# Attention scores on two 64-row tiles of the PE array instead of the full array with a block-diagonal K

## The chip, the cores and the metric

One core of one Trainium2 chip runs the whole kernel. The metric is device time in microseconds, the median of several executions. Engine names are those of the profile: PE is the matrix engine, PEld its weight loads, DVE, ACT and POOL the three element-wise engines, SP the engine that issues DMA.

## The reference, cut to what matters

```python
k_p = k.reshape(B, H, Sp, 8, D).mean(axis=3)            # B=8, H=8, Sp=72, D=64
v_p = v.reshape(B, H, Sp, 8, D).mean(axis=3)
scores = (q @ k_p.transpose(0, 1, 3, 2)) / sqrt(D)      # q: (8, 8, 576, 64)
attn = softmax(scores)                                  # over 72 pooled keys
x = (attn @ v_p) as (4608, 512)
out = gelu_tanh(x @ w_in) @ w_out                       # 512 -> 2048 -> 512
```

The head dimension is 64, half of the 128 rows of the PE array. That is what the change is about. The MLP after the attention is by far the larger part of the work.

## The kernel before

The kernel works through nine groups of 512 tokens: 512 tokens of each of the eight batches, and one remainder group made of the last 64 tokens of all eight. While PE runs the MLP of one group, the attention of the next is woven in at fixed steps of the MLP by hooks. One **score group** is the scores of 128 tokens and 8 heads. Two heads share a full-array matmul: the stationary operand is q of a pair of heads (128 rows), and the moving operand is a block-diagonal K, half of it zeros.

```python
kbd = consts.tile([128, B, HP, 2, Sp], BF16, name="kbd")        # zeroed once with a memset

def scores(g, j):
    sc = psum.tile([128, 2, MAIN], F32, name="sc", tag="sc", bufs=2)       # two banks
    for pr in range(HP):                                                   # 4 pairs of heads
        o = sc[:, pr // 2, 2 * Sp * (pr % 2):2 * Sp * (pr % 2) + 2 * Sp]
        if g < B:
            nc.tensor.matmul(out=o, lhsT=qT[:, j, pr, :], rhs=kbd[:, g, pr] ..., start=True, stop=True)
        else:                                          # remainder group: 64 tokens of two batches
            for half in range(2):
                p0 = 64 * half
                nc.tensor.matmul(out=o[p0:p0 + 64], lhsT=qT[:, j, pr, p0:p0 + 64],
                                 rhs=kbd[:, 2 * j + half, pr] ..., start=True, stop=True)

def exps(g, j):      # ACT: e = exp(sc / 64), 128 x 576
def norm(g, j, eng): # DVE: den = sum, r = 1/den; eb = e * r in bf16
...
# steady state: step 0 to 63 are the matmuls with w_in, 64 to 127 those with w_out
at(hooks, [67, 69, 78, 82][j], scores, n, j)
at(hooks, [67, 69, 78, 82][j], exps, n, j)
# first MLP
at(hooks, 16, first_t, 2)      # PE transposes of e, then a DVE copy
at(hooks, 32, first_t, 3)
at(hooks, 42, first_v)         # fourth cast of w_in on DVE, then the values
```

The softmax here doesn't subtract the row's maximum and nothing guards it: scores larger than these inputs give would overflow.

## Time and profile before

| what | before |
|---|---|
| median time | 301.14 us (301.05 to 301.31, 3 runs) |
| span of the profile | 299.3 us |
| PE busy, share of the span | 97% |
| one steady period (one group of 512 tokens) | 30.36 us, PE busy throughout |
| score group on PE, ordinary / remainder | 0.25 us / 0.47 us |

The lines are in the prediction below. How to read them: in the steady state PE has no gap at all, so the period is a sum of PE's slots, and anything that PE need not do is time gained. A slot is the distance between the starts of two neighbouring matmuls. Durations of single matmuls in the profile are modelled and longer than a slot, because matmuls are pipelined. At the start of the program PE waits for loads and casts, and there the sum of PE's work is not the measure.

### The profile page before, as it was taken

What the parts mean: (1) busy time and instruction counts of PE and PEld (TensorE: products, weight loads), DVE (VectorE), ACT (ScalarE), POOL (GpSimd) and SP (SyncE); (2) the same over time, 40 slices, a digit from 0 to 9 for tenths busy, and PEclk for the clock granted to TensorE, in tenths of its full rate; (3) what the DMA queues carried; (4) which work ended last, traced back from release to release, by engine and by line L of the source; (5) the groups of instructions that cost most, each with busy time, mean ns of one, the idle gap of its engine ahead of it and who ended that gap; (6) DMA issues with size and microseconds to landing.
All of it is one profiled execution on the core that took longest, in us unless ns stands there. A gap on an engine that the chain in (4) does not pass through costs nothing.

```text
span 299.3 us, 4581 instructions
## 1 busy us (share of the span) xinstructions
PE 290.7 (97%) x1734; PEld 151.6 (51%) x1734; DVE 146.7 (49%) x241; ACT 158.2 (53%) x242; POOL 55.5 (19%) x71
## 2 busy tenths in 40 slices
PE   7869999999999999999999999999999999999996
PEld 7748844445444544454445444544444544444444
DVE  6895769164706570648073807381639100920012
ACT  1477783667157715672477246724773267426500
POOL 3252033230400240024012400240024000100000
PEclk9999999999999999999999999999999999999999
DMA  7999997995699459947993599049944800351012
GB/s 235 357 387 338 384 350 132 343 279 158 135 279 250 145 127 271 269 146 126 261 297 134 119 249 301 4 107 249 276 147 101 164 36 2 79 114 37 0 70 70
DMA packets 73221, 56.32 MB, mean 188 GB/s; under 512 B 45808, under 2 KB 55408, under 8 KB 73200
## 3 DMA queue, kind: packets, MB, share of 16 engines
q1 hardware_dynamic: 73056, 55.98, 68.2%
q8 instruction: 13, 0.21, 0.3%
q10 hardware_dynamic: 144, 0.07, 0.1%
q14 instruction: 8, 0.07, 0.1%
HBM read 36.70 MB, written 9.44 MB: 154 GB/s over the span
## 4 chain that ended last, share of the span: by engine, by line
PE 91%; DMA 3%; DVE 2%; SPq 1%; POOL 1%; issue 0%; POOLq 0%
PE mm L296 41%; PE mm L301 41%; PE xo L266 4%; DMA q_sb<-in_q_dram 3%; PE sc L208 2%; PE mm L329 1%; POOL eb L231 1%; SPq L98 1%; PE xo L272 1%; PE tp L193 1%; PE sc L213 0%; DVE w_in_b L80 0%; PE tp L240 0%; DVE w_out_b L80 0%; POOL q_b L80 0%; PE xo L255 0%
## 5 line engine op out<-in xcount | busy, mean ns | idle before, releaser
L301 PE MATMUL mm<-w_out_b,gT 128*128 128x512 bf16 x560 | 128.6, 379 | 0.5 <-DVE w_out_b L80 0.5
L296 PE MATMUL mm<-xT,w_in_b 128*128 128x512 bf16 (+1 forms) x640 | 127.6, 358 | 0.5 <-DVE xT L80 0.5
L298 ACT ACTIVATE gT<-mm 128x512 bf16<-128x512 f32 (+1 forms) x160 | 88.4, 555 | 47.0 <-PE mm L296 45.9
L296 PEld LDWEIGHTS <-w_in_b 128*128 128x128 bf16 x640 | 62.2, 98 | 62.6 <-issue 0.5
L301 PEld LDWEIGHTS <-gT 128*128 128x128 bf16 x560 | 53.4, 98 | 59.7 <-DVE w_out_b L80 0.7
L80 DVE COPY osb<-mm 128x512 f32<-128x512 f32 (+2 forms) x37 | 24.3, 658 | 62.9 <-PE mm L301 60.8
L78 ACT CAST xT<-xo 128x1024 bf16<-128x1024 f32 (+1 forms) x18 | 16.6, 966 | 56.8 <-PE xo L266 49.1
L228 DVE TENSOR_REDUCE den<-e 128x8 f32<-128x576 f32 x36 | 26.5, 736 | 38.0 <-ACT e L221 37.9
L148 POOL TENSOR_TENSOR vbd<-kvb,vmask 128x256 bf16<-128x256 bf16 (+2 forms) x40 | 21.2, 553 | 113.5 <-DVE kvb L130 113.4
L128 DVE TENSOR_TENSOR kv<-kv 128x1024 f32<-128x1024 f32 (+3 forms) x20 | 22.4, 1118 | 29.7 <-DMA kv<-in_v_dram 27.7
L231 DVE TENSOR_TENSOR eb<-e,r 128x576 bf16<-128x576 f32 x28 | 27.2, 970 | 1.0
L221 ACT ACTIVATE e<-sc 128x576 f32<-128x576 f32 x36 | 22.5, 650 | 9.6 <-ACT e L221 4.0
L231 POOL TENSOR_TENSOR eb<-e,r 128x576 bf16<-128x576 f32 x8 | 10.1, 1266 | 71.5 <-ACT e L221 41.1
L80 POOL CAST q_b<-q_sb 128x2048 bf16<-128x2048 f32 (+1 forms) x7 | 15.0, 2147 | 4.1 <-DMA q_sb<-in_q_dram 4.1
L208 PEld LDWEIGHTS <-qT 128*128 128x128 bf16 x128 | 10.1, 98 | 7.0 <-ACT qT L78 0.6
L208 PE MATMUL sc<-kbd,qT 128*128 128x144 bf16 x128 | 13.2, 226 | 0.2 <-ACT qT L78 0.2
L266 PE MATMUL xo<-eT,vbd 128*128 128x512 bf16 x56 | 13.2, 379 | 0.0
L129 DVE TENSOR_TENSOR kv<-kv 128x512 f32<-128x512 f32 (+3 forms) x20 | 12.8, 640 | 0.7
L410 PE MATMUL warm<-identb 128*128 128x128 bf16 x112 | 9.1, 249 | 1.4 <-POOL vmask L398 1.4
L494 ACT ACT_TABLE_LOAD x8 | 10.3, 1283 | 0.1
L80 DVE COPY kbd<-kTd 64x288 bf16<-64x288 bf16 x12 | 5.6, 467 | 8.3 <-DMA kTd<-kvb 8.2
L314 ACT ACT_TABLE_LOAD x7 | 9.0, 1283 | 0.1
(55 smaller groups left out, 99.5 us busy)
## 6 DMA issues: line engine op xcount, KB each, us to landing
out_dram<-osb SPq DMA_DIRECT2D x31, 256.0 KB, 6.7
kv<-in_k_dram SPq DMA_DIRECT2D x7, 1024.0 KB, 6.5
q_sb<-in_q_dram SPq DMA_DIRECT2D x7, 1024.0 KB, 5.9
kv<-in_v_dram SPq DMA_DIRECT2D x7, 1024.0 KB, 9.9
w_in_s<-in_moe_w_in_dram SPq DMA_DIRECT2D x4, 1024.0 KB, 13.0
w_out_s<-in_moe_w_out_dram SPq DMA_DIRECT2D x4, 1024.0 KB, 13.8
out_dram<-osb SPq DMA_DIRECT2D x9, 128.0 KB, 2.3
kv<-in_k_dram SPq DMA_DIRECT2D x2, 512.0 KB, 3.9
```

Of the source, the lines that this page charges most:

```text
L78: eng.copy(out=out, in_=in_)
L80: eng.tensor_copy(out=out, in_=in_)
L128: add(out=t[:, :, 0:4, :], in0=t[:, :, 0:4, :], in1=t[:, :, 4:8, :], op=ALU.add)
L148: eng.tensor_tensor(out=vbd[p0:128, b, n0:n1, :].rearrange("p (c r) (hh d) -> p c (r hh) d", c=max(m, 1), d=D), in0=kvb[p0:128, 4 + c0:4 + ...
L208: nc.tensor.matmul(out=o, lhsT=qT[:, j, pr, :], rhs=kbd[:, g, pr].rearrange("d hh s -> d (hh s)"), start=True, stop=True)
L221: nc.scalar.activation(out=e.rearrange("p (x h) s -> p x (h s)", x=2), in_=sc[:, :, 0:4 * Sp], func=ACT.Exp, scale=1.0 / 64.0)
L228: nc.vector.reduce_sum(out=den, in_=e, axis=AX.X)
L231: eng.tensor_tensor(out=eb[:, j, 128 * 5 - W:].rearrange("p (h s) -> p h s", s=Sp), in0=e, in1=r.unsqueeze(2).to_broadcast([128, H, Sp]), ...
L266: nc.tensor.matmul(out=xo[:, i, :], lhsT=vbd[:, g, n, :], rhs=eT[:, :, c, :], start=(x == 0), stop=(x == 1))
L296: nc.tensor.matmul(out=hp[:, 0:c1 - c0], lhsT=w_in_b[:, ko, fo * 128:(fo + 1) * 128], rhs=st[g]["xT"][:, ko, c0:c1], start=(ko == 0), stop ...
L298: nc.scalar.activation(out=gT[:, fo, c0:c1], in_=hp[:, 0:c1 - c0], func=ACT.Gelu_apprx_tanh)
L301: nc.tensor.matmul(out=o, lhsT=gT[:, fo, r * 128:(r + 1) * 128], rhs=w_out_b[:, fo, :], start=(fo == 0), stop=(fo == FO - 1))
```

## The change

The intent: half of each score matmul multiplies zeros. The PE array can be used as two tiles of 64 rows, with the even head of a pair on one and the odd head on the other at the same time. Then K needs no zeros, and a pair of heads takes 72 columns instead of 144. The two tiles are kept from writing one PSUM bank together (the prediction says on what that rests): even heads go to one bank and odd heads to the other, and the normalisation puts the heads back in order as it writes. Three hooks of the first MLP move as well. The core of the diff:

```diff
-    kbd = consts.tile([128, B, HP, 2, Sp], BF16, name="kbd")
+    kh = consts.tile([128, B, HP, Sp], BF16, name="kh")
...
         for pr in range(HP):
-            o = sc[:, pr // 2, 2 * Sp * (pr % 2):2 * Sp * (pr % 2) + 2 * Sp]
-            if g < B:
-                nc.tensor.matmul(out=o, lhsT=qT[:, j, pr, :], rhs=kbd[:, g, pr] ..., start=True, stop=True)
...
+            for hh in range(2):
+                h0 = 64 * hh
+                o = sc[:, hh, Sp * pr:Sp * pr + Sp]
+                if g < B:
+                    nc.tensor.matmul(out=o, lhsT=qT[h0:h0 + 64, j, pr, :], rhs=kh[h0:h0 + 64, g, pr],
                                      start=True, stop=True)
+                else:
+                    for p0 in (0, 64):
+                        nc.tensor.matmul(out=o[p0:p0 + 64], lhsT=qT[h0:h0 + 64, j, pr, p0:p0 + 64],
+                                         rhs=kh[h0:h0 + 64, 2 * j + p0 // 64, pr], start=True, stop=True)
...
-        eng.tensor_tensor(out=eb[...].rearrange("p (h s) -> p h s", s=Sp), in0=e, ...)
+        eng.tensor_tensor(out=eb[...].rearrange("p (pr hh s) -> p hh pr s", hh=2, s=Sp), in0=e, ...)
...
-    nc.vector.memset(kbd, 0.0)
...
-    at(hooks, 16, first_t, 2)
-    at(hooks, 32, first_t, 3)
-    at(hooks, 42, first_v)
+    at(hooks, 28, first_t, 2)
+    at(hooks, 38, first_t, 3)
+    at(hooks, 48, first_v)
```

More of the change, by code (lines that the diff above doesn't have):

```diff
@@ L184, in k_spread @@
             src = st[b]["kT"][p0:p0 + 64, 0:W].rearrange("d (pr hh s) -> d hh pr s", hh=2, s=Sp)[:, hh]
-            copy(engs[hh], kbd[p0:p0 + 64, b, :, hh, :], src)
+            copy(engs[hh], kh[p0:p0 + 64, b], src)
     def qT_tile(g):
@@ L205, in scores @@
         for pr in range(HP):
-            o = sc[:, pr // 2, 2 * Sp * (pr % 2):2 * Sp * (pr % 2) + 2 * Sp]
-            if g < B:
-                nc.tensor.matmul(out=o, lhsT=qT[:, j, pr, :], rhs=kbd[:, g, pr].rearrange("d hh s -> d (hh s)"),
-                                 start=True, stop=True)
-            else:
-                for half in range(2):
-                    p0 = 64 * half
-                    nc.tensor.matmul(out=o[p0:p0 + 64], lhsT=qT[:, j, pr, p0:p0 + 64],
-                                     rhs=kbd[:, 2 * j + half, pr].rearrange("d hh s -> d (hh s)"),
+            for hh in range(2):
[3 more added lines that the diff above has]
+                    nc.tensor.matmul(out=o, lhsT=qT[h0:h0 + 64, j, pr, :], rhs=kh[h0:h0 + 64, g, pr],
                                      start=True, stop=True)
+                else:
+                    for p0 in (0, 64):
+                        nc.tensor.matmul(out=o[p0:p0 + 64], lhsT=qT[h0:h0 + 64, j, pr, p0:p0 + 64],
+                                         rhs=kh[h0:h0 + 64, 2 * j + p0 // 64, pr], start=True, stop=True)
         st[g][("sc", j)] = sc
@@ L219, in exps @@
         sc = st[g].pop(("sc", j))
-        e = work.tile([128, H, Sp], F32, name="e", bufs=4)
-        nc.scalar.activation(out=e.rearrange("p (x h) s -> p x (h s)", x=2), in_=sc[:, :, 0:4 * Sp],
+        e = work.tile([128, 2, HP, Sp], F32, name="e", bufs=4)
+        nc.scalar.activation(out=e.rearrange("p hh pr s -> p hh (pr s)"), in_=sc[:, :, 0:4 * Sp],
                              func=ACT.Exp, scale=1.0 / 64.0)
@@ L226, in norm @@
         e = st[g][("e", j)]
-        den = work.tile([128, H], F32, name="den")
+        den = work.tile([128, 2, HP], F32, name="den")
         nc.vector.reduce_sum(out=den, in_=e, axis=AX.X)
-        r = work.tile([128, H], F32, name="r")
+        r = work.tile([128, 2, HP], F32, name="r")
         nc.vector.reciprocal(out=r, in_=den)
-        eng.tensor_tensor(out=eb[:, j, 128 * 5 - W:].rearrange("p (h s) -> p h s", s=Sp), in0=e,
-                          in1=r.unsqueeze(2).to_broadcast([128, H, Sp]), op=ALU.mult)
+        eng.tensor_tensor(out=eb[:, j, 128 * 5 - W:].rearrange("p (pr hh s) -> p hh pr s", hh=2, s=Sp),
+                          in0=e, in1=r.unsqueeze(3).to_broadcast([128, 2, HP, Sp]), op=ALU.mult)
     def eT_tile(g):
```

## The prediction

> **What bounds the kernel now.** I read the page top down: engine shares, slices, chain. Then I read one period of the steady state in the windows view, and then the timeline of PE around each kind of score group, because the change acts there.
>
> ```profile
> PE 290.7 (97%) x1734; PEld 151.6 (51%) x1734; DVE 146.7 (49%) x241; ACT 158.2 (53%) x242; POOL 55.5 (19%) x71
> PEclk9999999999999999999999999999999999999999
> PE mm L296 41%; PE mm L301 41%; PE xo L266 4%; DMA q_sb<-in_q_dram 3%; PE sc L208 2%; PE mm L329 1%; POOL eb L231 1%; SPq L98 1%; PE xo L272 1%; PE tp L193 1%; PE sc L213 0%; DVE w_in_b L80 0%; PE tp L240 0%; DVE w_out_b L80 0%; POOL q_b L80 0%; PE xo L255 0%
> ...
> 115.81:146.17 30.36, 30.36 (x154) 14.20 (x152) 15.68 (x24) 16.54 (x24) 6.03 (x7) 1.00 0.78 200
> ```
>
> The reader is to see that PE is the bound, at full clock, and that scores (L208, L213) are under 3% of the chain. In one steady period of 30.36 us PE is busy for all 30.36 while DVE and ACT have half of it free: the period is 64 + 64 matmuls of 512 columns and 8 of the values at 0.216 us (13.81 us for 64 in the chain in order of time), 29.35 us, plus four score groups of 0.25 us, 1.0 us. So whatever the change does to the time PE needs for a score group appears one for one in the total, and whatever it does to DVE, ACT or POOL there is hidden. The start is different: PE waits there, and the change also moves hooks there.
>
> What a score group costs PE is read from starts, since ends of matmuls are modelled:
>
> ```profile
> 100.01 0.59 PE L301 MATMUL mm<-w_out_b,gT 128*128 128x512 bf16 x2
> 100.44 0.41 PE L208 MATMUL sc<-kbd,qT 128*128 128x144 bf16 x4
> 100.69 0.59 PE L301 MATMUL mm<-w_out_b,gT 128*128 128x512 bf16 x2
> ...
> 220.52 0.81 PE L301 MATMUL mm<-w_out_b,gT 128*128 128x512 bf16 x3
> 221.26 0.44 PE L213 MATMUL sc<-kbd,qT 128*64 128x144 bf16 x8
> 221.64 0.60 PE L301 MATMUL mm<-w_out_b,gT 128*128 128x512 bf16 x2
> ```
>
> ```profile
> 32.69 0.52 PE L174 MATMUL kT<-identb,kvb 128*128 128x128 bf16 x5
> 33.00 0.09 PEld L174 LDWEIGHTS <-kvb 64*128 64x128 bf16 x1
> 33.13 0.10 PEld L296 LDWEIGHTS <-w_in_b 128*128 128x128 bf16 x1
> 33.14 0.28 PE L296 MATMUL mm<-xT,w_in_b 128*128 128x256 bf16 x1
> ...
> 34.02 0.39 PE L193 MATMUL tp<-identb,q_b 128*128 128x128 bf16 x4
> 34.24 0.27 PE L296 MATMUL mm<-xT,w_in_b 128*128 128x256 bf16 x1
> ...
> 234.73 2.03 PE L272 MATMUL xo<-eT,vbd 128*128 128x64 bf16 x64
> 236.60 0.60 PE L301 MATMUL mm<-w_out_b,gT 128*128 128x512 bf16 x2
> ```
>
> First fence: an ordinary group (full array, four matmuls of 144 columns) takes 100.69 - 100.44 = 0.25 us, 62.5 ns each. The remainder group (L213) uses 64-column tiles. PE could have begun it at 220.52 + 3 x 0.216 = 221.17; the next full-array matmul starts at 221.64. That is 0.47 us, though two tiles side by side need only four slots of 62.5 ns, 0.25 us: **0.22 us are lost** on the way into the tile shape and out of it. Second fence: the fifth K transpose has 64 rows (64*128), which is the very shape that the change uses. Four full transposes take 0.22 us (34.02 to 34.24), and a 64-column matmul takes 1.87/64 = 0.029 us (234.73 to 236.60), so five should take 0.25. They take 33.14 - 32.69 = 0.45: **0.20 us are lost**. The weight load at 33.00 comes some 0.09 us after the fourth transpose has streamed, and the next full-array load waits again. No semaphore explains it: the operand was ready at 32.66 by the DVE rows.
>
> **What the Trainium skill says.** "TensorEngine Tiling (Array Packing)", Key Properties: "Mode switching requires drain", for a change of mode and not of tile alone. The trace agrees, with 0.20 and 0.22 us for a visit. The same page, Gotcha 1: different row tiles must not write one PSUM bank at once; hence the layout with even heads in one bank and odd heads in the other. No run yet shows it. "TensorE: Matmul & The Clock Gate", Back-to-back issue gap: about N/2.4 + 2.5 ns for each warm matmul. The trace agrees at 144 columns (62.5) and at 64 (29). For 72 columns it gives an estimate of 32.5 ns. The same page, Part 3: matmuls on different row groups start about 4 ns apart. No run here shows this for rows; for columns the remainder group agrees, since its eight matmuls fit only if they run in pairs.
>
> **The change part by part.** (1) Ordinary score groups. Four full matmuls of 144 columns become eight of 64 rows and 72 columns, with eight weight loads. In pairs on the two row tiles they need 4 x 32.5 = 0.13 us, plus the visit, 0.20 to 0.22: about 0.34 us for 0.25, so **+0.09 us a group**. The half that concurrency saves (0.12 us) is less than one visit costs, because each group stands alone between full-array matmuls. Of the 32 ordinary groups four are in the prologue, and two more (at 37.32 and 37.67) stand just ahead of a wait of 0.50 us of PE for the w_out_b cast, which takes in their extra. 26 x 0.09 to 0.10 = **+2.5 us**.
>
> (2) Remainder groups, four. They pay for a visit already. Sixteen matmuls on four 64x64 tiles, four at a time: 4 x 32.5 + 0.22 = 0.35 for 0.47: -0.1 each, **-0.4 us** at best.
>
> (3) The memset of kbd goes (1.98 us of DVE at 1.35). DVE then waits 0.87 us for the first K load anyway: 0.
>
> (4) exp reads the same two times 288 columns. The normalisation writes with a four-dimensional pattern: the same elements on DVE, off the chain in the steady state: 0. The copies of K become contiguous: hidden.
>
> (5) Prologue. Each of the four groups is later by about 0.1; the first feeds a dense DVE chain, the last an ACT copy that PE needs at 19.5: **+0.1 us**.
>
> (6) The hooks. The first e transpose moves from step 16 to 28, the second from 32 to 38.
>
> ```profile
> 22.38 0.45 PE L240 MATMUL tp<-identb,eb 128*128 128x128 bf16 x5 [1.19 <-POOL eb L231]
> 22.67 1.91 PE L296 MATMUL mm<-xT,w_in_b 128*128 128x256 bf16 x16
> 24.42 0.44 PE L240 MATMUL tp<-identb,eb 128*128 128x128 bf16 x5
> 24.82 0.39 PE L296 MATMUL mm<-xT,w_in_b 128*128 128x256 bf16 x2
> ```
>
> This looks like a gain of 1.19 us, PE's wait for the POOL normalisation: 12 matmuls of 0.109 us now fill it. But step 32 needs the third w_in cast, which POOL does right after (22.83 to 24.76, started by a DMA). In the kernel before, PE reaches step 32 at 24.82, just behind that cast. After the change PE gets to step 32 at about 23.1 and waits for the same cast until 24.8. So the wait moves rather than goes, and the second transposition (0.28 us), which used to lie ahead of this join, now lies behind it: **+0.3 us**.
>
> Sum: 2.5 - 0.4 + 0.1 + 0.3 = +2.5 us, 301.1 + 2.5 = 303.6. I put 303.8, a little higher, for the chance that the pairs do not overlap fully.
>
> **Rivals.** (a) The row tiles do not overlap (weight loads or the fast weight path hold them apart): 8 x 32.5 = 0.26 us, 0.13 more for each of 26 groups, +3.4 us: about 307. Against: the column pairs of L213 overlap, and loads with their 64-column matmuls go at 29 ns in L272. For: L213's loads have 64 columns, these have 128 on two row tiles, which no instruction before shows. (b) Row tiles switch cheaply and the intent holds: 0.13 us a group, -0.12 x 30 = -3.6 us, about 297.5. Against: the 64-row transpose paid in full. (c) The hooks win their 1.19 us, if the third w_in cast comes earlier or its data did: about 302.4. Against: that cast starts on a DMA landing that the change does not touch. (d) POOL's normalisation with four-dimensional patterns gets much slower than 2.08 us and delays the same cast: +0.5 to 1 us at the start. No measurement speaks for or against it, and the later hooks may have been set for it.
>
> **Range and chances.** (a) halfway gives 305.5, (c) gives 302.4; a range of 302.0 to 306.6 holds these. Slower by over 2% needs 307.2, (a) in full: 0.07. Faster by over 2% needs 295.1, which even (b) misses: 0.01. Within 2%: 0.92.
>
> **What would show it.** Right: steady periods of about 30.7 us instead of 30.36; each score group taking 0.34 us from the slot it could take to the next matmul of L302, with about 0.09 us before its first weight load; pairs a few ns apart and 32 ns between pairs; remainder groups shorter than before; in the first MLP a PE wait of over 1 us for the w_in cast in place of the one for eb. Wrong: groups of 0.25 us or less (no drain for rows), starts evenly 32 ns apart (no pairs), or a first score-free stretch of the MLP that begins earlier than before.

## The result, and the profile after

| | before | after |
|---|---|---|
| median | 301.10 us (300.98 to 301.31, 4 runs) | 303.31 us (303.12 to 303.35, 4 runs) |
| ratio | | 1.0071, 95% interval 1.0054 to 1.0089 |
| steady period | 30.36 us | 30.72 us |
| period with the remainder's scores | 31.40 us | 30.94 us |

Ratios here and below are the mean time of one kernel's fast runs over the mean of the other's fast runs of the same rounds, so they are not quite the ratio of the medians quoted. Periods are the distance between the starts of two neighbouring MLPs in the trace; read from single starts or from the chain, they differ by 0.01 to 0.02 us.

The page of the changed kernel (engine shares) and its windows view for one steady period (length, then busy time of PE, PEld, DVE, ACT and POOL, granted clock, DMA share, GB/s):

```profile
PE 292.2 (97%) x1894; PEld 146.4 (49%) x1894; DVE 145.0 (48%) x240; ACT 158.0 (52%) x242; POOL 55.1 (18%) x71
...
86.06:116.78 30.72, 30.72 (x170) 13.68 (x168) 15.86 (x24) 16.55 (x24) 6.03 (x7) 1.00 0.75 201
```

PE has 160 matmuls more and is still the bound: busy for all 30.72 us of a period that is 0.36 us longer. Four score groups a period make that +0.09 us each. The timeline of PE around an ordinary score group (L210), with its weight loads (PEld), and a remainder group (L214) says where they come from; the columns are start, length, engine, line, operation, tiles, array shape and count:

```profile
99.93 0.59 PE L302 MATMUL mm<-w_out_b,gT 128*128 128x512 bf16 x2
100.45 0.18 PEld L210 LDWEIGHTS <-qT 64*128 64x128 bf16 x8 [0.42 <-issue]
100.45 0.30 PE L210 MATMUL sc<-kh,qT 64*128 64x72 bf16 x8
100.69 0.61 PE L302 MATMUL mm<-w_out_b,gT 128*128 128x512 bf16 x2
...
222.60 0.81 PE L302 MATMUL mm<-w_out_b,gT 128*128 128x512 bf16 x3
223.34 0.33 PE L214 MATMUL sc<-kh,qT 64*64 64x72 bf16 x16
223.59 0.60 PE L302 MATMUL mm<-w_out_b,gT 128*128 128x512 bf16 x2
```

PE could have begun the score group two slots of 0.216 after 99.93, at 100.36. It begins at 100.45, so 0.09 us pass with nothing streaming. The next full-array matmul starts at 100.69: 0.33 us for the group, where it was 0.25. The eight matmuls do run in pairs: single starts in the trace are 100.454 and 100.458, then 100.493 and 100.496, 100.527 and 100.530, 100.559 and 100.563. The pairs are 32 to 39 ns apart, and the two of a pair 3 to 4 ns. So the concurrency is there, and it is the way in and out that costs. The way out can be read too: the last pair starts at 100.563, so its stream ends at about 100.595 (an estimate, with a slot of 32 ns), and the next full-array weight load is recorded at 100.686, again 0.09 us later. In the kernel before, the first weight load of a group is recorded at 100.22, 0.22 us ahead of its matmul at 100.44; here the first load of each shape starts with its own matmul, at 100.45 and at 100.69. Whether the visit's price is a drain of the array or these loads that are no longer issued ahead, no run separates. The remainder group, which switched shape before as well, went from 0.47 to 223.59 - 223.25 = 0.34 us.

The first MLP after, for the four lines that the prediction shows of before:

```profile
22.31 0.44 PE L241 MATMUL tp<-identb,eb 128*128 128x128 bf16 x5
22.59 0.60 PE L297 MATMUL mm<-xT,w_in_b 128*128 128x256 bf16 x4
24.43 0.83 PE L297 MATMUL mm<-xT,w_in_b 128*128 128x256 bf16 x6 [1.24 <-POOL w_in_b L80]
25.10 0.44 PE L241 MATMUL tp<-identb,eb 128*128 128x128 bf16 x5
```

The wait of 1.19 us for the POOL normalisation (eb) is gone, and a wait of 1.24 us for the third cast of w_in stands in its place. The second transposition is now behind that wait.

The two traces add up. From before to after: -0.38 us until PE begins the first MLP (luck of the run, as the hooks' section shows), +0.61 in the first MLP, six ordinary periods of +0.37 (2.2), -0.46 in the remainder's period. The sum is +1.97 us, which is the difference of the spans (299.29 and 301.26).

### The profile page after: what moved, and what is told of

The parts are those of the page before. It is cut to its first block, busy times and chain, and to the rows that moved or that the text cites. A ratio compares the mean times of both kernels' runs of the same rounds, so it can differ in the third digit from the quotient of the medians.

```text
span 301.3 us, 4900 instructions
## 1 busy us (share of the span) xinstructions
PE 292.2 (97%) x1894; PEld 146.4 (49%) x1894; DVE 145.0 (48%) x240; ACT 158.0 (52%) x242; POOL 55.1 (18%) x71
## 4 chain that ended last, share of the span: by engine, by line
PE 90%; DMA 4%; SPq 3%; ACT 1%; POOL 1%; issue 0%; DVE 0%; ACTq 0%
PE mm L302 41%; PE mm L297 40%; DMA w_in_s<-in_moe_w_in_dram 4%; PE xo L267 4%; PE sc L210 2%; SPq L378 1%; PE mm L330 1%; SPq L98 1%; POOL w_in_b L80 1%; PE xo L273 1%; ACT L344 0%; SPq L110 0%; PE sc L214 0%; PE tp L193 0%; PE xo L256 0%
## 5 line engine op out<-in xcount | busy, mean ns | idle before, releaser
L302 PEld LDWEIGHTS <-gT 128*128 128x128 bf16 x560 | 52.2, 98 | 60.7 <-DVE w_out_b L80 0.5
L232 POOL TENSOR_TENSOR eb<-e,r 128x576 bf16<-128x576 f32 x8 | 10.1, 1266 | 74.7 <-ACT e L222 44.2
L210 PEld LDWEIGHTS <-qT 64*128 64x128 bf16 x256 | 5.8, 96 | 12.4 <-issue 11.4
L210 PE MATMUL sc<-kh,qT 64*128 64x72 bf16 x256 | 9.7, 197 | 0.4 <-ACT e L222 0.2
L80 DVE COPY kh<-kTd 64x288 bf16<-64x288 bf16 x12 | 5.6, 471 | 6.5 <-DMA kTd<-kvb 6.3
```

What stands on the lines that cost most here:

```text
L80: eng.tensor_copy(out=out, in_=in_)
L210: nc.tensor.matmul(out=o, lhsT=qT[h0:h0 + 64, j, pr, :], rhs=kh[h0:h0 + 64, g, pr], start=True, stop=True)
L232: eng.tensor_tensor(out=eb[:, j, 128 * 5 - W:].rearrange("p (pr hh s) -> p hh pr s", hh=2, s=Sp), in0=e, in1=r.unsqueeze(3).to_broadcast([ ...
L302: nc.tensor.matmul(out=o, lhsT=gT[:, fo, r * 128:(r + 1) * 128], rhs=w_out_b[:, fo, :], start=(fo == 0), stop=(fo == FO - 1))
```

## The experiments

My theory: a **visit** of PE to another tile shape costs about 0.21 us, whatever stands in it; inside, a slot of 72 columns costs 32 ns and the two row tiles overlap. The main rival: the doubled number of matmuls and weight loads is what costs. All kernels of the table gave outputs that passed the comparison, but that comparison is weak for the scores. One kernel with wrong scores for the odd heads (below) passed too, because these scores are so small that the softmax is nearly even. So it doesn't vouch for the order of the heads.

| run | edit | median us | ratio to before (95%) | steady period |
|---|---|---|---|---|
| two visits | groups after the first MLP's cut in two | 309.47 | 1.0275 (1.026 to 1.0291) | 31.57 |
| shared visit | two groups back to back | 300.48 | 0.9976 (0.996 to 0.9993) | 30.30 |
| full array, 72 columns | before, matmuls halved | 301.60 | 1.0015 (1.0 to 1.003) | 30.40 |
| one tile after the other | loops swapped | 304.04 | 1.0097 (1.0082 to 1.0112) | 30.76 |
| one row tile only | wrong | 307.37 | 1.0213 (1.0197 to 1.0228) | 31.23 |
| old hooks | change without its hooks | 303.24 | 1.0071 (1.0059 to 1.0084) | 30.72 |
| new hooks | before with the hooks | 301.39 | 1.0015 (1.0003 to 1.0028) | 30.35 |
| memset kept | change with the memset | 303.46 | 1.0078 (1.0065 to 1.0092) | 30.72 |
| shared, all | shared visits, old hooks | 299.66 | 0.9955 (0.9942 to 0.9967) | 30.30 |
| before, groups paired | control | 300.86 | 0.9991 (0.9978 to 1.0003) | 30.36 |

The kernel before, in the rounds of these runs, had medians of 301.07 to 301.15 us.

### Two visits for one

```diff
-                at(hooks, [67, 69, 78, 82][j], scores, n, j)
+                at(hooks, [67, 69, 78, 82][j], scores, n, j, (0, 1))
+                at(hooks, [68, 70, 79, 83][j], scores, n, j, (2, 3))     # same matmuls, one L302 matmul between
```

> The changed kernel, but each of the 28 score groups after the first MLP's (24 of 64-row tiles, 4 of the remainder) is cut in two halves with one full-array matmul of L302-kind between them: the same instructions, twice the visits to the tile shape. Theory (a visit costs about 0.21 us of PE whatever stands in it): +28 x 0.21 = +5.9 us against the changed kernel, about 309.2, each steady period 31.56 instead of 30.72. Rival (the extra cost of the change is the doubled number of matmuls and weight loads, not the visit): no change, about 303.3.

Measured: 309.47 us. The windows view of a period, and the timeline of two half groups:

```profile
118.96:150.53 31.57, 31.57 (x169) 13.97 (x168) 15.62 (x24) 16.54 (x24) 6.02 (x7) 1.00 0.76 196
...
101.78 0.24 PE L212 MATMUL sc<-kh,qT 64*128 64x72 bf16 x4
101.95 0.39 PE L303 MATMUL mm<-w_out_b,gT 128*128 128x512 bf16 x1
102.27 0.24 PE L212 MATMUL sc<-kh,qT 64*128 64x72 bf16 x4
```

The matmuls are the same, and the period is 31.57 - 30.72 = 0.85 us longer for four more visits: 0.21 us each. Each visit is seen: from 101.78 to 102.27 pass 0.49 us, of which 0.216 are the one full-array matmul and about 0.065 two pairs.

### Two groups in one visit

```diff
-                at(hooks, [67, 69, 78, 82][j], scores, n, j)
-                at(hooks, [67, 69, 78, 82][j], exps, n, j)
+                at(hooks, [68, 68, 80, 80][j], scores, n, j)
+                at(hooks, [68, 68, 80, 80][j], exps, n, j)
```

> The changed kernel, but in the steady state two score groups stand back to back, at steps 68 and 80, so two groups share one visit: 14 visits fewer. Theory (visit 0.21 us): -14 x 0.21 = -2.9 us against the changed kernel, about 300.4, steady period about 30.30, a little under both kernels, if the second group of a visit need not wait for a PSUM buffer. Rival (number of instructions): no change, about 303.3.

Measured: 300.48 us. A period and a double group:

```profile
85.89:116.19 30.30, 30.30 (x170) 13.68 (x168) 15.62 (x24) 16.43 (x24) 6.03 (x7) 1.00 0.76 202
...
100.50 0.43 PE L210 MATMUL sc<-kh,qT 64*128 64x72 bf16 x16
100.87 0.39 PE L302 MATMUL mm<-w_out_b,gT 128*128 128x512 bf16 x1
```

Two visits fewer in a period take 0.42 us off it, 0.21 us each again. With one, two and half a visit to a group the time lies on a straight line, with the same instructions each time. More than two groups at once would need more PSUM: a group holds two banks, and there are two such buffers. In this run's remainder period PE waited besides (0.3 us, for a transposition of e by DMA), which the last version below did not show.

### The instruction count without the tile shape

```diff
-                nc.tensor.matmul(out=o, lhsT=qT[:, j, pr, :], rhs=kbd[:, g, pr].rearrange("d hh s -> d (hh s)"), ...)
+                for hh in range(2):
+                    nc.tensor.matmul(out=o[:, Sp * hh:Sp * hh + Sp], lhsT=qT[:, j, pr, :], rhs=kbd[:, g, pr, hh], ...)
```

> The kernel before with K still block-diagonal and the full array, but every ordinary score matmul of 144 columns cut into two of 72, each with its own weight load: the instruction count of the change without its tile shape. Theory (only the visit costs): eight slots of 32.5 ns, 0.26 us for 0.25, so 28 x 0.01 = +0.3 us against before, about 301.4. Rival (doubled instructions cost what the change lost): +0.09 us a group, +2.5 us, about 303.5.

Measured: 301.60 us, with a period of 30.40.

```profile
99.68 0.42 PE L209 MATMUL sc<-kbd,qT 128*128 128x72 bf16 x8
99.94 0.60 PE L302 MATMUL mm<-w_out_b,gT 128*128 128x512 bf16 x2
```

Eight matmuls and eight loads on the full array take 0.26 us. Twice the instructions cost 0.01 us a group, not 0.09. The rival falls.

### What the concurrency is worth, and who makes it

```diff
# one row tile only (wrong result on purpose: odd heads read the even heads' rows)
-                h0 = 64 * hh
+                h0 = 0
# one tile after the other
-        for pr in range(HP):
-            for hh in range(2):
+        for hh in range(2):
+            for pr in range(HP):
```

> Wrong result on purpose: the changed kernel with the odd heads also read from partitions 0 to 63, so that all eight matmuls of a group go to one row tile and cannot overlap; same visits, same instruction count. Theory (the pairs overlap fully in the changed kernel): eight slots of 32.5 ns instead of four, +0.13 us for each of 26 exposed ordinary groups and less for the remainder, +3.4 to +3.9 us against the changed kernel, about 306.9; steady period 31.24. Rival (the pairs hardly save anything): about 303.3.

> The changed kernel with the loops swapped: all four even heads on the upper row tile first, then all four odd heads on the lower one, so that no two neighbours can run side by side but at the one crossing. Theory (the pairs overlap fully in the changed kernel, and PE starts matmuls in program order): about 7 slots instead of 4, +0.1 us for each of 26 exposed groups, +2.5 us against the changed kernel, about 305.8. Rival (the order does not matter, both tiles are fed independently): no change, about 303.3.

Measured: 307.37 us for one row tile only, and 304.04 us for one tile after the other. First the group in the kernel with one row tile, then in the kernel with swapped loops:

```profile
101.50 0.43 PE L210 MATMUL sc<-kh,qT 64*128 64x72 bf16 x8
101.86 0.39 PE L302 MATMUL mm<-w_out_b,gT 128*128 128x512 bf16 x1
```

```profile
100.92 0.31 PE L210 MATMUL sc<-kh,qT 64*128 64x72 bf16 x8
101.17 0.61 PE L302 MATMUL mm<-w_out_b,gT 128*128 128x512 bf16 x2
```

On one tile a group takes 0.36 us from first start to next full-array matmul, against 0.24 in the changed kernel, and the period is 31.23 - 30.72 = 0.51 us longer. That is 0.13 us a group, four slots of 32 ns: the pairs overlap fully.

The swapped loops did **not** do what I expected. I had expected 305.8 and the period of a nearly serial group; the period is 30.76, only 0.01 us a group above the changed kernel. My step "PE starts matmuls in program order" fell. In the trace the starts come in pairs here too (100.923 and 100.936, 100.961 and 100.974, and so on). In the program the wait for the second half of K stands on the fifth matmul, the first on the lower tile; in the trace the matmul with that wait is the second to start. PE had gone past three matmuls of the upper tile. As this trace records it, each row tile worked through its own matmuls. The periods account for 0.3 of the 0.7 us between this median and the changed kernel's. In the two profiles, whose spans differ by 1.08 us, the rest lies in the start (PE began the first MLP at 19.33 us, not at 18.88) and in the end (0.33 us more after the last MLP has begun); why is not shown.

### The hooks and the memset

```diff
# old hooks: in the changed kernel          # new hooks: in the kernel before
-    at(hooks, 28, first_t, 2)              -    at(hooks, 16, first_t, 2)
-    at(hooks, 38, first_t, 3)              -    at(hooks, 32, first_t, 3)
-    at(hooks, 48, first_v)                 -    at(hooks, 42, first_v)
+    at(hooks, 16, first_t, 2)              +    at(hooks, 28, first_t, 2)
+    at(hooks, 32, first_t, 3)              +    at(hooks, 38, first_t, 3)
+    at(hooks, 42, first_v)                 +    at(hooks, 48, first_v)
# memset kept: in the changed kernel
+    kz = consts.tile([128, B, HP, 2, Sp], BF16, name="kz")
+    nc.vector.memset(kz, 0.0)
```

> The changed kernel with the three hooks of the first MLP back at steps 16, 32 and 42. Theory (the wait for the POOL normalisation only moves to the wait for the third w_in cast, and the second e transposition now lies behind that join): 0.3 us less than the changed kernel, about 303.0. Rival (the later hooks gain the 1.2 us that PE waited): 1.2 us more, about 304.5.

> The kernel before with the hooks of the change alone (28, 38, 48). Theory: +0.3 us against before, about 301.4, with the wait of PE at the third w_in cast. Rival (hooks gain): -1.2 us, about 299.9.

> The changed kernel with the memset of 128x2304 words put back, to a buffer that nothing reads. In the profiles PE starts the first MLP at 18.88 us in the changed kernel and at 19.26 before, with the q load landing 0.4 us sooner. Theory (DVE waits for the K load anyway; the landing varies from run to run): no change, within 0.1 us of 303.3. Rival (the memset holds up the start): +0.4 us, about 303.7, the first MLP at 19.26 again.

Measured: 303.24, 301.39 and 303.46 us. The medians agree with a loss of 0.3 us by the new hooks and rule out a gain of 1.2, but 0.3 us is close to their spread. The trace is sharper, if one counts from the start of the first MLP to the start of the second. The windows views of that stretch, each from its own kernel: before, after, old hooks, new hooks.

```profile
19.26:54.94 35.68, 33.95 (x255) 23.00 (x255) 26.38 (x48) 24.41 (x45) 9.38 (x8) 1.00 0.98 313
```

```profile
18.88:55.17 36.29, 34.31 (x271) 22.42 (x271) 26.46 (x48) 24.30 (x45) 9.19 (x9) 1.00 1.00 316
```

```profile
19.20:55.16 35.96, 34.22 (x271) 22.61 (x271) 26.46 (x48) 24.28 (x45) 9.17 (x8) 1.00 0.98 315
```

```profile
19.79:55.76 35.97, 34.01 (x256) 22.88 (x256) 26.38 (x48) 24.40 (x45) 9.44 (x8) 1.00 0.98 310
```

The new hooks lengthen the stretch by 35.97 - 35.68 = 0.29 us on the old scores and by 36.29 - 35.96 = 0.33 us on the new ones, and the scores lengthen it by about as much again (0.28 and 0.32). Single profiles vary: the four that have the changed kernel's first MLP (the change, memset kept, two visits, shared visit) gave 36.17 to 36.40 us, so each difference is good to about 0.1. A steadier measure runs from PE's start of the first MLP to its first matmul with w_out: 19.30 to 19.44 us in the five profiles with the old hooks, 19.64 to 19.88 in the seven with the new ones. No profile with the new hooks was faster there.

PE's start of the first MLP lay between 18.88 and 19.79 us over the twelve profiles, with no tie to the change: with the memset kept it came at 18.96, and with the old kernel's scores and the new hooks at 19.79. So the 0.38 us by which the changed kernel was early in its profile belong to the run, to the landing of its loads, and not to the missing memset: in eleven of the twelve profiles PE began 4.5 to 4.6 us after POOL began the first cast of q, which itself waits for q's load.

### A layout

I also built the changed kernel with both heads of a pair in one PSUM bank, as the kernel before lays them out. The check ahead of the chip refused it, as two row tiles would write one bank with nothing to order them. So no run shows what that part of the change is worth; that it can't be left out rests on that check.

### A version that beats both, and its control

```diff
# in the changed kernel: the shared visits above, the hooks of the kernel before, and in the first MLP
-        at(hooks, [126, 127, 136, 140][j], scores, 1, j)
-        at(hooks, [128, 128, 136, 140][j], exps, 1, j)
+        at(hooks, [126, 126, 140, 140][j], scores, 1, j)
+        at(hooks, [128, 128, 140, 140][j], exps, 1, j)
# control: the kernel before with its score groups at [68, 68, 80, 80]
```

> Score groups two to a visit everywhere after the prologue (steps 68 and 80 of the steady state, 126 and 140 of the first MLP), and the hooks of the kernel before (16, 32, 42). Theory: the kernel with shared visits took 300.48; the hooks give 0.3 back and one more exposed visit goes, 0.2: about 300.0, under both kernels. Rival (the start, where PE waits on loads and casts, takes it back): 300.5.

> Control: the kernel before with its score groups moved to steps 68 and 80 in the same way. Full-array groups have no visit to share. Theory: no change, 301.1, steady period 30.36. Rival (the new places of the groups themselves gain, whatever the tile shape): about 300.4 or lower.

Measured: 299.66 us for the version and 300.86 for the control; the steady periods are in the table.

The control's steady period didn't move, as full-array groups have no visit to share; its remainder period did, from 31.40 to 30.94, because the remainder's column tiles are a visit too: two fewer, 0.23 us each. The version is 0.45% under the kernel before and faster than the change by 3.6 us. Its steady period gains only about 0.05; the larger gain is in the remainder's period (31.40 to 30.55, of which the control has about half), 0.2 us are in the first MLP, and some of the profile's lead over before (0.37 us) is again the start of the run.

## Why the prediction was right

**The bound and the path.** Right: PE stayed the bound without a gap in the steady state, and the longer groups appeared one for one in the period.

**A visit of 0.20 to 0.22 us, read from the remainder group and the 64-row transpose.** Right, and shown by taking visits away and adding them: 0.21 us either way. The line that carried most was a single transpose in the first MLP that already used the new shape.

**Ordinary groups, +0.09 us each.** Right in size: +0.092. I counted 26 exposed groups, +2.5 us. The 24 of the steady state gave 2.2. The two in the first MLP gave about 0.3 rather than 0.2 (from the first matmul with w_out to the second MLP, 16.52 us for 16.24): one of them waits 0.22 us, by the timeline, for the exp that frees its PSUM buffer. That the two groups ahead of the w_out_b wait cost nothing held: from PE's start of the first MLP to the end of that wait passed 19.44 us before, and 19.44 again with the new scores and the old hooks.

**Remainder groups, -0.1 each.** Right: -0.46 us for the four together, -0.4 predicted.

**Memset, exp, normalisation, copies: 0.** Right: keeping the memset changed nothing clear of noise (303.46), and the four-dimensional normalisation on POOL took as long as before (mean 1266 ns on both pages), so rival (d) is out.

**The hooks, +0.3.** Right, and the least obvious point: the wait of 1.19 us for eb only turned into one of 1.24 us for the cast of w_in.

**Prologue, +0.1.** Not settled: the start varies by 0.9 us between profiles, which hides it.

**The rivals.** (a) The pairs do overlap: one row tile only cost 0.13 us a group more. (b) fell with the first trace, (c) with the hooks' runs. The sum for (c) was off: with a gain of 1.19 in place of the loss of 0.3 my terms give 302.1, not 302.4, which the range still held. The 0.2 us that I added for (a) was not needed: my sum of terms was 303.6, and 303.31 was measured, inside the range.

## What to carry to other kernels

Price a change of the array's shape as a visit, here 0.21 us for going in and coming out, and set it against what the smaller tiles save inside: one group of four pairs saved 0.12 us and lost, two groups together broke even, and only work that had paid for a visit already gained outright. Look in the profile of the kernel that you have for an instruction that already uses the new form, however small, because its neighbours' start times give the price before anything is written. And when a wait is to be filled by moving work, look for what the same engine does next: here the consumer only met the next instruction of the same POOL queue.

## What the Trainium skill lacked or had wrong

- "TensorEngine Tiling (Array Packing)", Key Properties, says that a change of mode drains but gives no price, and its table of theoretical speedup leaves it out. Here: 0.21 us for in and out together (0.85 us for four more visits), of which 0.09 us pass between the end of the last full-array stream and the first weight load, and 0.09 again on the way out. A score group went from 0.25 to 0.33 us.
- "TensorE: Matmul & The Clock Gate", Part 3, has matmuls start and end in strict program order. Here, across two row tiles, the recorded starts did not keep it: with all upper-tile matmuls ahead of all lower-tile ones in the program, the group took 0.25 us, as in pairs (0.24), and not nearly the 0.36 us of one tile; the fifth matmul of the program started second.
- The same page, same Part, has weight loads overlap running matmuls only where the row group differs. Here, with one row tile alone, eight matmuls with eight loads kept slots of 32 to 39 ns, while that trace records 92 to 98 ns for each such load: they overlap on the same rows too, as that page's own step on weight loads (background buffer) allows.
- That page's gap of N/2.4 + 2.5 ns (Back-to-back issue gap) held at 72 columns, on the full array (0.26 us for eight) and on row tiles (32 ns). The page gives it for an isolated matmul, and for a sustained stream of loads and matmuls it gives 131 ns at 512 columns and 81 at 128; here such streams took 216 ns at 512 and 55 at 128 (four transposes in 0.22 us).
